# Weight units of an attention stage made in pieces, one per attention head, with the sign of a number carried by the slope of a leaky activation

## The chip, the cores and the metric

The kernel runs on one core of one Trainium2 chip. A core has five engines that run side by side and each take their own instructions in order: TensorE (PE in the profile; it multiplies matrices, and its weight loads are listed as PEld), VectorE (DVE), ScalarE (ACT), GpSimd (POOL) and SyncE (SP), which here issues all the transfers between the chip's memory (HBM) and the on-chip memory (SBUF). PSUM is the small memory into which TensorE writes its results; it has eight banks. Engines wait for each other by semaphores.

The metric is the time of one execution in microseconds (us) on the device. The kernel before took 622.03 us, the median of 3 runs (620.55 to 623.03).

## The reference

Three stages follow one another. q, k and v have 2 batches, 12 heads, 448 positions and a head size of 64, so there are 24 heads in all. The weights are float64 in memory, and the result is float32.

```python
def _attn_ref(q, k, v):                      # causal attention, all 24 heads
    scores = scale * np.matmul(q, k.transpose(0, 1, 3, 2))
    scores = np.where(mask, -1000000000.0, scores)
    attn = np.exp(scores - np.max(scores, axis=-1, keepdims=True))
    attn = attn / (np.sum(attn, axis=-1, keepdims=True) + 1e-09)
    return np.matmul(attn, v)
def _moe_ref(x, w_gate, w_val, w_out):       # 896 x 768, inner size 1536
    g = x @ w_gate
    silu = g * (1.0 / (1.0 + np.exp(-g)))
    val = x @ w_val
    return silu * val @ w_out
def _moe2_ref(x, w_in, w_out):               # 896 x 768, inner size 2048
    h = x @ w_in
    return (h * np.clip(h + 3.0, 0.0, 6.0) / 6.0) @ w_out
```

## The kernel before

**Precision.** A float32 product is made from three products of shortened numbers: each operand is split into a high part (float32r) and the rest. So every weight tile exists as `whi` and `wlo`.

**Weight units.** The weights are handled in 68 units of 128 x 768 numbers. `w_unit` makes one: SP loads the raw float64 bits (`raw`, 768 KB); ScalarE multiplies the upper word, read as a float32, by 2^-112 (L96), VectorE shifts the result left by 3 (L99), which throws the sign away, puts the sign bit back from the upper word (L100) and adds the top bits of the lower word (L103); ScalarE rounds to `whi` (L108), and GpSimd subtracts for `wlo` (L109). L100 and L103 both read two SBUF tiles, `raw` and `w`.

**Attention.** `attention()` goes through the heads in steps t = 0 to 27, one head per step, as a pipeline: in step t TensorE makes the scores of head t (`sc`, L315), the transposes of the probabilities of head t-1 (`tp`, L358) and the product with v of head t-2 (`pv`, L386). `weave` deals these products out in turn, so that TensorE's order is fixed by hand. In even steps the q and k of the next pair of heads are turned as well (`turn_parts`: four `kn` and four `qn` transposes, L241, copies `f` by ScalarE, CASTs by VectorE into `kk` and `qq` (L254), subtractions by GpSimd for the rest (L255), and for the keys two copies by transfer per head (L260)). In odd steps the finished outputs are turned (`xt_parts`, L420). For the scores of each head VectorE makes four reductions (L328, the tile `e`, one for each of the widths 336, 112, 224 and 448, in this order) and ScalarE four exponentials (L338). TensorE's transposes in step t+1 begin with the block of width 112 that comes from step t. Between the 336 and the 112 reduction stands the copy `et` (L364).

**Order.** A scheduler orders each engine's instructions by its own estimate of times, except those that are pinned to program order. Of the attention's weight units, the first instruction (L96) is pinned, the load is not. Three units are made in the attention stage, whole, after steps 20, 23 and 26 (`UNIT_AT`).

**MLPs.** `mlps()` then uses the units in order, two units ahead of use; all its products are matmuls of L168 and L529.

Of the kernel before, what the change touches and what calls it, by code (L numbers as in the profile page):

```python
# [8 lines left out]
F32 = mybir.dt.float32  # L9
F32R = mybir.dt.float32r  # L10
U32 = mybir.dt.uint32
AF = mybir.ActivationFunctionType
ALU = mybir.AluOpType
# [11 lines left out]
AHEAD = 2  # L25
SOON = 200
LATE = 2
UNIT_AT = (20, 23, 26)
GROUPS = ((2,), (0, 1), (3,))

@with_exitstack
def tile_attention_glu_mlp(
# [17 lines left out]
    nc = tc.nc  # L50
# [7 lines left out]
    KD = DM // 128  # L58
# [21 lines left out]
    def bank(use):  # L80
        n = idle.pop(0)
        return banks.tile([128, 512], F32, tag=f"bank{n}", name=f"{use}_{n}"), n


    def w_unit(src, a, b):
        def slot(tag, shape, dt, n, m):
            i = made_n[tag] = made_n.get(tag, -1) + 1
            i %= m if more else n
            return (ring if i < n else more[0]).tile(shape, dt, tag=f"{tag}{i}", name=f"{tag}{i}")

        raw = slot("raw", [128, a, b, 2], U32, RAW, RAW + 1)
        nc.sync.dma_start(out=raw.rearrange("p a b two -> p a (b two)"), in_=src)
        low, high = raw[:, :, :, 0], raw[:, :, :, 1]
        w = ring.tile([128, a, b], F32, tag="w", name="w", bufs=2)
        wu = w.bitcast(U32)
        first = nc.scalar.activation(out=w, in_=high.bitcast(F32), func=AF.Copy, scale=2.0**-112)  # L96
        if in_attention:
            tc.keep_in_program_order(first)
        nc.vector.tensor_scalar(out=wu, in0=wu, scalar1=3, scalar2=None, op0=ALU.logical_shift_left)  # L99
        nc.vector.scalar_tensor_tensor(  # L100
            out=wu, in0=high, scalar=0x80000000, in1=wu, op0=ALU.bitwise_and, op1=ALU.bitwise_or
        )
        nc.vector.scalar_tensor_tensor(  # L103
            out=wu, in0=low, scalar=29, in1=wu, op0=ALU.logical_shift_right, op1=ALU.bitwise_or
        )
        hi = slot("whi", [128, a, b], F32R, WB, WB + 1)
        lo = slot("wlo", [128, a, b], F32R, WB, WB + 1)
        nc.scalar.copy(hi, w)  # L108
        nc.gpsimd.tensor_tensor(out=lo, in0=w, in1=hi.bitcast(F32), op=ALU.subtract)  # L109
        return hi, lo  # L110

    def cols(w, j, n=128):
        w = w.bitcast(U32)
# [2 lines left out]
    units = []  # L116
# [13 lines left out]
    made = []  # L130
    made_n = {}
    more = []
    in_attention = [1]
    used = [0]

    def prefetch(n):
        while len(made) < min(n, len(units)):
            made.append(w_unit(*units[len(made)]))

    def next_unit():  # L140
        u = used[0]
# [36 lines left out]
    def attention():  # L178
        with ExitStack() as st:
# [9 lines left out]
                out=mask[:, S - C :], in_=mask[:, S - C :], pattern=[[-1, C]],  # L189
# [7 lines left out]
            for i in range(NV):  # L197
                t = fix.tile([C, 2, NC, D + 1], F32, name=f"v1_{i}")
# [8 lines left out]
            def load(p):  # L207
                if p >= NPAIR:
                    return
                b, hp = pairs[p]  # L210
                h0 = 2 * hp
                for src, dst, nm in ((k, natk, "kn"), (q, natq, "qn")):
                    t = nat.tile([C, NC, 2, D], F32, tag=nm, name=nm)
                    for j in range(2):
                        nc.sync.dma_start(  # L215
                            out=t[:, :, j, :], in_=src[b, h0 + j].rearrange("(c p) d -> p c d", p=C)
                        )
                    dst[p] = t

            def load_v(p):  # L220
                if p >= NPAIR:
                    return
                b, hp = pairs[p]
                vt = vset[p % NV]
                nc.sync.dma_start(
                    out=vt.rearrange("p j c d -> p (j c) d")[:, :, :D],
                    in_=v[b, 2 * hp : 2 * hp + 2].rearrange("j (c p) d -> p (j c) d", p=C),
                )

            def turn_parts(p):  # L230
                if p >= NPAIR:
                    return []
                t = sets[p % NSET]
                box = {}

                def one(src, c):
                    n = src[p]
                    if c == 0:
                        box["tr"] = bank("tr")
                    tr, bn = box["tr"]  # L240
                    nc.tensor.transpose(  # L241
                        tr[:, c * C : (c + 1) * C], n[:, c].rearrange("p j d -> p (j d)"), ident[:C, :C]
                    )
                    if c < NC - 1:
                        return
                    f = wk.tile([128, S], F32, tag="f", name="f")
                    nc.scalar.copy(f, tr[:, :S])
                    idle.append(bn)
                    hi, lo = (t["qq"], t["qq"]) if src is natq else (t["kk"], t["k2"])
                    for j in range(2):  # L250
                        r = slice(j * 64, j * 64 + 64)
                        o = slice(64 - j * 64, 128 - j * 64)
                        lr = o if src is natq else r
                        nc.vector.tensor_copy(hi[r, j, :], f[r, :])  # L254
                        nc.gpsimd.tensor_tensor(  # L255
                            out=lo[lr, j, :], in0=f[r, :], in1=hi[r, j, :].bitcast(F32), op=ALU.subtract
                        )
                        if src is natk:
                            for w in (hi, lo):
                                nc.sync.dma_start(out=w[o, j, :].bitcast(F32), in_=w[r, j, :].bitcast(F32))  # L260

                return [lambda src=src, c=c: one(src, c) for src in (natk, natq) for c in range(NC)]

            def first_turn():

                t = sets[0]
                got = {}
                for nm, src in (("k", natk), ("q", natq)):
                    got[nm] = bank("tr")
                    for c in range(NC):  # L270
                        nc.tensor.transpose(
                            got[nm][0][:, c * C : (c + 1) * C],
                            src[0][:, c].rearrange("p j d -> p (j d)"),
                            ident[:C, :C],
                        )
                kt, qt = (got[nm][0][:, :S] for nm in "kq")

                def head(j):
                    r = slice(j * 64, j * 64 + 64)
                    o = slice(64 - j * 64, 128 - j * 64)  # L280
                    kk, k2, qq = (t[nm][:, j, :] for nm in ("kk", "k2", "qq"))
                    nc.vector.tensor_copy(kk[r], kt[r])
                    nc.vector.tensor_tensor(out=k2[r], in0=kt[r], in1=kk[r].bitcast(F32), op=ALU.subtract)
                    nc.scalar.copy(qq[r], qt[r])
                    nc.gpsimd.tensor_copy(kk[o], kk[r].bitcast(F32))
                    nc.vector.tensor_tensor(out=qq[o], in0=qt[r], in1=qq[r].bitcast(F32), op=ALU.subtract)
                    nc.scalar.copy(k2[o], k2[r].bitcast(F32))
                    if j == 1:
                        idle.extend(n for _, n in got.values())

                head(0)
                return [lambda: head(1)]
# [136 lines left out]
            def weave(*lists):  # L429
                marked = sorted(  # L430
                    ((i + 0.5) / len(l) + 1e-3 * k, k, i) for k, l in enumerate(lists) for i in range(len(l))
                )
                for _, k, i in marked:
                    lists[k][i]()
# [2 lines left out]
            load(1)  # L437
            load_v(0)
            second = first_turn()
            for t in range(0, NH + 4):  # L440
                turns_now = []
                if t % 2 == 0:
                    nxt = t // 2 + 1
                    turns_now = turn_parts(nxt)
                    load(nxt + 1)
                    load_v(nxt)
                if t % 2 == 1:
                    turns_now = xt_parts((t - 5) // 2)
                weave(sc_parts(t), tp_parts(t - 1), pv_parts(t - 2), turns_now, second)
                second = []  # L450
                if t in UNIT_AT:
                    prefetch(UNIT_AT.index(t) + 1)

    def mlps():
        in_attention.clear()
        more.append(ctx.enter_context(tc.tile_pool(name="more", bufs=1)))
        gpool = ctx.enter_context(tc.tile_pool(name="gpool", bufs=1))

# [29 lines left out]
        for e in range(KD):  # L488
            got = [bank("mm") for _ in PARTS]
            pts = [t[:, : part.stop - part.start] for (t, _), part in zip(got, PARTS)]  # L490
            for hh in range(2):
                wh, wl = next_unit()
                for pt, part in zip(pts, PARTS):
# [3 lines left out]
                        first=hh == 0,  # L497
# [37 lines left out]
        for eh in range(2):  # L535
            got = [bank("mm") for _ in range(TT)]
            acc = [t[:, :EH] for t, _ in got]
            for g in range(NG - LATE):
                w = next_unit()
# [15 lines left out]
            idle.extend(n for _, n in got)  # L555

    attention()
    mlps()


# [28 lines left out]
```

## Time and profile before

| | us |
|---|---|
| median of 3 runs | 622.03 |
| the profiled execution: its own time | 623.78 |
| the profiled execution: span, first to last instruction | 622.0 |
| TensorE busy in the span | 610.7 (98%) |
| VectorE busy | 344.8 (55%) |
| ScalarE busy | 265.2 (43%) |
| GpSimd busy | 185.6 (30%) |

The attention stage takes the first 123 us of the span, the two MLPs the rest. The table's shares are means over both: a share of 55% for VectorE says nothing of the attention stage, where it is much higher. What matters for a change in one stage is which wait ends last there, and that is read from the timeline of that stage, engine by engine. A step's start is read from the first score product of the step (L315, 128x336).

### The profile page before, as it was taken

The numbers are of one execution on the slowest core, as the hardware profiler recorded it, in microseconds if no ns is written. First come the engines' busy times: TensorE is split into PE (matmuls) and PEld (weight loads), VectorE is DVE, ScalarE is ACT, GpSimd is POOL, SyncE is SP. The second block draws the span as 40 slices with busy tenths as digits, with TensorE's granted clock in tenths as the row PEclk, the third lists the DMA queues.
The fourth block names the chain that finished last, engine by engine and source line by source line (L and its number), as shares of the span: only waits on it lengthen the run. The fifth ranks groups of instructions, "written<-read, shape, count | busy, mean of one in ns | idle before, by whom it ended". The sixth has DMA issues, their size and how long they took to land.

```text
span 622.0 us, 9356 instructions
## 1 busy us (share of the span) xinstructions
PE 610.7 (98%) x3600; PEld 565.9 (91%) x3600; DVE 344.8 (55%) x687; ACT 265.2 (43%) x450; POOL 185.6 (30%) x125
## 2 busy tenths in 40 slices
PE   6999998999999999999999999999999999999997
PEld 5999998989988889998888999888899999999997
DVE  5788889669855544444544343566666543325101
ACT  5777777544443334333322323554555442223100
POOL 4456655025322222322222232222223222213200
PEclk9999999799999999999999999999999999999999
DMA  9665542146543333333333334333334433352002
GB/s 179 187 158 130 140 112 70 44 152 203 156 149 103 102 103 115 127 112 101 102 101 102 108 117 127 106 103 102 101 103 110 126 119 101 102 166 77 0 1 89
DMA packets 83916, 70.14 MB, mean 113 GB/s; under 512 B 35232, under 2 KB 79776, under 8 KB 83872
## 3 DMA queue, kind: packets, MB, share of 16 engines
q1 hardware_dynamic: 83872, 69.55, 38.9%
q8 instruction: 28, 0.46, 0.3%
q14 instruction: 16, 0.13, 0.1%
HBM read 61.73 MB, written 2.75 MB: 104 GB/s over the span
## 4 chain that ended last, share of the span: by engine, by line
PE 93%; DVE 3%; DMA 1%; ACT 1%; SPq 1%; issue 0%; ACTq 0%; DVEq 0%
PE mm L168 60%; PE mm L529 19%; PE pv L386 5%; PE sc L315 4%; PE tp L358 3%; PE tr L241 1%; DMA kk<-kk 1%; PE tr L420 1%; DVE e L328 1%; SPq L215 1%; DMA qn<-in_q_dram 1%; DVE qq L254 1%; DVE w L100 0%; DVE w L103 0%; ACT e L338 0%
## 5 line engine op out<-in xcount | busy, mean ns | idle before, releaser
L109 POOL TENSOR_TENSOR wlo<-w,whi 128x768 fp32r<-128x768 f32 x68 | 128.0, 1884 | 359.1 <-ACT whi L108 298.4
L99 DVE TENSOR_SCALAR w<-w 128x768 uint32<-128x768 uint32 x68 | 38.7, 570 | 156.0 <-ACT w L96 155.7
L108 ACT CAST whi<-w 128x768 fp32r<-128x768 f32 x68 | 56.9, 839 | 124.1 <-PE mm L168 83.7
L168 PE MATMUL mm<-x1l,whi 128*128 128x384 f32 (+1 forms) x288 | 104.9, 364 | 0.2 <-DVE x1l L151 0.2
L168 PE MATMUL mm<-x1h,wlo 128*128 128x384 f32 (+1 forms) x288 | 104.9, 364 | 0.0
L96 ACT ACTIVATE w<-raw 128x768 f32<-128x768 f32 x68 | 61.3, 902 | 101.4 <-POOL wlo L109 98.9
L168 PE MATMUL mm<-x1h,whi 128*128 128x384 f32 (+1 forms) x288 | 104.5, 363 | 0.0
L103 DVE SCALAR_TENSOR_TENSOR w<-raw,w 128x768 uint32<-128x768 uint32 x68 | 74.6, 1097 | 1.0
L386 PE MATMUL pv<-v,et 112*112 112x65 f32 x480 | 75.2, 246 | 0.0
L529 PE MATMUL mm<-whi,gl 128*128 128x384 f32 x224 | 74.8, 334 | 0.0
L529 PE MATMUL mm<-whi,gh 128*128 128x384 f32 x224 | 74.8, 334 | 0.0
L529 PE MATMUL mm<-wlo,gh 128*128 128x384 f32 x224 | 74.8, 334 | 0.0
L168 PE MATMUL mm<-x2h,wlo 128*128 128x384 f32 (+1 forms) x192 | 70.0, 364 | 0.0
L168 PE MATMUL mm<-x2l,whi 128*128 128x384 f32 (+1 forms) x192 | 69.8, 364 | 0.0
L168 PE MATMUL mm<-x2h,whi 128*128 128x384 f32 (+1 forms) x192 | 69.6, 362 | 0.0
L386 PEld LDWEIGHTS pv<-v,et 112*112 112x112 f32 x480 | 67.8, 182 | 1.6
L100 DVE SCALAR_TENSOR_TENSOR w<-raw,w 128x768 uint32<-128x768 uint32 x68 | 65.9, 968 | 1.6
L358 PE MATMUL tp<-ident,e 112*112 112x112 f32 x240 | 63.3, 272 | 2.2 <-ACT e L338 2.0
L168 PEld LDWEIGHTS mm<-x1l,whi 128*128 128x128 f32 x288 | 54.0, 188 | 6.5 <-DVE x1l L151 0.5
L168 PEld LDWEIGHTS mm<-x1h,whi 128*128 128x128 f32 x288 | 54.1, 188 | 6.2 <-ACT x1h L150 0.2
L168 PEld LDWEIGHTS mm<-x1h,wlo 128*128 128x128 f32 x288 | 54.0, 188 | 5.6
L338 ACT ACTIVATE e<-e,m 112x336 f32<-112x336 f32 (+1 forms) x96 | 48.8, 532 | 22.7 <-DVE m L328 22.7
(69 smaller groups left out, 1050.0 us busy)
## 6 DMA issues: line engine op xcount, KB each, us to landing
raw<-in_moe_w_out_dram SPq DMA_DIRECT2D x28, 768.0 KB, 4.3
raw<-in_moe_w_in_dram SPq DMA_DIRECT2D x16, 768.0 KB, 4.5
raw<-in_moe_w_gate_dram SPq DMA_DIRECT2D x12, 768.0 KB, 4.3
raw<-in_moe_w_val_dram SPq DMA_DIRECT2D x12, 768.0 KB, 4.3
kn<-in_k_dram SPq DMA_DIRECT2D x24, 112.0 KB, 2.9
qn<-in_q_dram SPq DMA_DIRECT2D x24, 112.0 KB, 2.6
v<-in_v_dram SPq DMA_DIRECT2D x12, 224.0 KB, 3.1
out_dram<-ob SPq DMA_DIRECT2D x14, 192.0 KB, 1.8
```

Of the source, the lines that this page charges most:

```text
L96: first = nc.scalar.activation(out=w, in_=high.bitcast(F32), func=AF.Copy, scale=2.0**-112)
L99: nc.vector.tensor_scalar(out=wu, in0=wu, scalar1=3, scalar2=None, op0=ALU.logical_shift_left)
L100: nc.vector.scalar_tensor_tensor(out=wu, in0=high, scalar=0x80000000, in1=wu, op0=ALU.bitwise_and, op1=ALU.bitwise_or)
L103: nc.vector.scalar_tensor_tensor(out=wu, in0=low, scalar=29, in1=wu, op0=ALU.logical_shift_right, op1=ALU.bitwise_or)
L108: nc.scalar.copy(hi, w)
L109: nc.gpsimd.tensor_tensor(out=lo, in0=w, in1=hi.bitcast(F32), op=ALU.subtract)
L168: lambda lhs=lhs, rhs=rhs, i=i: nc.tensor.matmul(ps, lhs, rhs, start=(first and i == 0), stop=(last and i == total - 1))
L315: nc.tensor.matmul(sp[:C, o : o + w], t["qq"][:, j, c * C : (c + 1) * C], t[("kk", "k2")[i]][:, j, 0:w], start=(i == 0), stop=(i == 1),)
L338: nc.scalar.activation(out=es, in_=es, func=AF.Exp, scale=-1.0, bias=m[:, x : x + 1])
L358: nc.tensor.transpose(tp[:C, at - lo : at - lo + C], e[:, at : at + C], ident[:C, :C])
L386: nc.tensor.matmul(box["o"][:, qc, :], et[:, at : at + C], vt[:, j, c, :], start=(c == 0), stop=(c == qc))
L529: nc.tensor.matmul(acc, lhs[:, tsl], rhs[:, i, :], start=(fc == 0 and n == 0), stop=(fc == K2 - 1 and n == 2),)
```

## The change

Three things change. First, the scaling by ScalarE becomes a leaky activation with the slope 2^32 for negative numbers: a negative number comes out with 32 more in its exponent, and the shift left by 3 moves just this bit to the place of the sign. The VectorE instruction that put the sign back (L100) is gone, in all 68 units. Second, units in the attention stage are made in pieces: the first two in 6 pieces of 128 columns, the third in 2 of 384. After each step at most one piece (or the load) is emitted. Third, the units start after steps 11, 18 and 25; their load, their scaling and their shift are pinned to program order.

```diff
-UNIT_AT = (20, 23, 26)
+UNIT_AT = (11, 18, 25)
...
-        first = nc.scalar.activation(out=w, in_=high.bitcast(F32), func=AF.Copy, scale=2.0**-112)
-        if in_attention:
-            tc.keep_in_program_order(first)
-        nc.vector.tensor_scalar(out=wu, in0=wu, scalar1=3, scalar2=None, op0=ALU.logical_shift_left)
-        nc.vector.scalar_tensor_tensor(
-            out=wu, in0=high, scalar=0x80000000, in1=wu, op0=ALU.bitwise_and, op1=ALU.bitwise_or
-        )
...
+        def load():
+            first = nc.sync.dma_start(out=raw.rearrange("p a b two -> p a (b two)"), in_=src)
+            if pieces > 1:
+                tc.keep_in_program_order(first)
+
+        def piece(k):
+            p = slice(k * a // pieces, (k + 1) * a // pieces)
+            low, high, wu = raw[:, p, :, 0], raw[:, p, :, 1], w[:, p].bitcast(U32)
...
+            first = nc.scalar.activation(
+                out=w[:, p], in_=high.bitcast(F32), func=AF.Prelu, scale=2.0**-112, alpha=2.0**32
+            )
+            if pieces > 1:
+                tc.keep_in_program_order(first)
+            shift = nc.vector.tensor_scalar(out=wu, in0=wu, scalar1=3, scalar2=None, op0=ALU.logical_shift_left)
+            if pieces > 1:
+                tc.keep_in_program_order(shift)
+            nc.vector.scalar_tensor_tensor(
+                out=wu, in0=low, scalar=29, in1=wu, op0=ALU.logical_shift_right, op1=ALU.bitwise_or
+            )
+            nc.scalar.copy(hi[:, p], w[:, p])
+            nc.gpsimd.tensor_tensor(out=lo[:, p], in0=w[:, p], in1=hi[:, p].bitcast(F32), op=ALU.subtract)
...
                 if t in UNIT_AT:
-                    prefetch(UNIT_AT.index(t) + 1)
+                    pieces += w_unit(*units[len(made)], pieces=KD if len(made) < 2 else 2)
+                if pieces:
+                    pieces.pop(0)()
```

A piece that is emitted after step t runs in step t+1: the first unit's pieces in steps 13 to 18, the second's in steps 20 to 25. All lines of the kernel move down by 13 (L254 becomes L267, L328 becomes L341); L99 becomes L114, L103 becomes L117, L109 becomes L121 and the load L92 becomes L100.

The first place is VectorE in step 21, an odd step, from the reciprocal to the 112 reduction; before:

```order
L398 RECIPROCAL ri<-r 112x4
L254 CAST qq_98<-f 64x448 x2
L399 TENSOR_TENSOR xn<-pv_1572,ri 112x4x64
L328 ISA e,m<-sc_1668,mask 112x336
L328 ISA m 112x1
L364 COPY et<-tp_1666 112x336
L99 TENSOR_SCALAR w<-w 128x768
L100 SCALAR_TENSOR_TENSOR w<-raw_1650,w 128x768
L328 ISA e,m<-sc_1680,mask 112x112
```

The same place on VectorE now:

```order
L411 RECIPROCAL ri<-r 112x4
L267 CAST qq_98<-f 64x448 x2
L412 TENSOR_TENSOR xn<-pv_1617,ri 112x4x64
L341 ISA e,m<-sc_1707,mask 112x336
L341 ISA m 112x1
L114 TENSOR_SCALAR w<-w 128x128
L377 COPY et<-tp_1705 112x336
L117 SCALAR_TENSOR_TENSOR w<-raw_1542,w 128x128
L341 ISA e,m<-sc_1719,mask 112x112
```

The piece stands where the whole unit stood, one of its two instructions ahead of the copy `et` and one behind it, and still in front of the 112 reduction. Steps 13, 15 and 17 now read the same; before they had no weight instructions.

The second place is GpSimd, over the same part of the attention stage; before, three pairs of heads and then the first unit:

```order
L255 TENSOR_TENSOR k_94<-f,kk_93 64x448 x2
L255 TENSOR_TENSOR qq_92<-f,qq_92 64x448 x2
L255 TENSOR_TENSOR k_97<-f,kk_96 64x448 x2
L255 TENSOR_TENSOR qq_95<-f,qq_95 64x448 x2
L255 TENSOR_TENSOR k_100<-f,kk_99 64x448 x2
L255 TENSOR_TENSOR qq_98<-f,qq_98 64x448 x2
L109 TENSOR_TENSOR wlo_1658<-w,whi_1657 128x768
```

GpSimd now, in steps 15 to 17:

```order
L268 TENSOR_TENSOR qq_98<-f,qq_98 64x448 x2
L121 TENSOR_TENSOR wlo_975<-w,whi_974 128x128
L268 TENSOR_TENSOR k_94<-f,kk_93 64x448
L121 TENSOR_TENSOR wlo_975<-w,whi_974 128x128
L268 TENSOR_TENSOR k_94<-f,kk_93 64x448
L268 TENSOR_TENSOR qq_92<-f,qq_92 64x448 x2
```

One piece of an odd step stands ahead of the two key subtractions, and one of an even step between them.

The third place is SP, which issues the transfers; before, the second unit's load stood here, in step 4:

```order
L225 DMA v_0_101<-in_v_dram 112x8x64
L92 DMA raw_1838<-in_moe_w_val_dram 128x6x256
L260 DMA kk_93<-kk_93 64x448
L260 DMA k_94<-k_94 64x448
L260 DMA kk_93<-kk_93 64x448
L260 DMA k_94<-k_94 64x448
L215 DMA kn<-in_k_dram 112x4x64 x2
```

SP now, where the first unit is loaded, behind the key copies of step 10:

```order
L273 DMA kk_93<-kk_93 64x448
L273 DMA k_94<-k_94 64x448
L273 DMA kk_93<-kk_93 64x448
L273 DMA k_94<-k_94 64x448
L100 DMA raw_972<-in_moe_w_gate_dram 128x6x256
L228 DMA qn<-in_q_dram 112x4x64 x2
L238 DMA v_1_103<-in_v_dram 112x8x64
L228 DMA kn<-in_k_dram 112x4x64 x2
```

The load stood right ahead of a pair's key copies; now it stands right behind them, with the input loads of later pairs behind it. TensorE's order is the same as before but for two places of a few rows.

## Rows read from the trace of the kernel before

**Rows 1.** Waits, whole span: engine, line, what for; us, times, longest

```profile
PE tp L358 <- ACT e L338: 2.0, 2, 1.6
```

**Rows 2.** Windows: stretch, length, busy time (instructions) by engine, clock, DMA, GB/s

```profile
65.48:74.27 8.79, 8.79 (x91) 8.60 (x90) 7.81 (x30) 6.65 (x16) 4.98 (x5) 1.00 0.56 129
...
108.54:115.27 6.73, 6.73 (x36) 6.41 (x37) 3.55 (x15) 3.37 (x7) 1.53 (x1) 0.50 0.32 110
...
304.00:618.50 314.50, 314.50 (x1652) 293.79 (x1651) 138.20 (x198) 107.74 (x160) 73.80 (x40) 1.00 0.33 99
```

**Rows 3.** Timeline of TensorE, steps 5, 17, 18, 21, 22: start, length, instruction, [idle before]

```profile
29.72 0.39 PE L315 MATMUL sc<-kk,qq 128*112 128x336 f32 x1
34.47 0.38 PE L315 MATMUL sc<-kk,qq 128*112 128x336 f32 x1 [0.30 <-DMA kk<-kk]
...
83.07 0.39 PE L315 MATMUL sc<-kk,qq 128*112 128x336 f32 x1
...
87.28 0.39 PE L315 MATMUL sc<-kk,qq 128*112 128x336 f32 x1
...
100.67 0.39 PE L315 MATMUL sc<-kk,qq 128*112 128x336 f32 x1
...
106.57 0.31 PE L358 MATMUL tp<-ident,e 112*112 112x112 f32 x1 [1.57 <-ACT e L338]
106.67 0.38 PE L315 MATMUL sc<-kk,qq 128*112 128x336 f32 x1
```

**Rows 4.** Timeline of VectorE in step 17, an odd step without a unit

```profile
83.61 1.12 DVE L254 CAST qq<-f 64x448 fp32r<-64x448 f32 x2
...
85.52 0.50 DVE L364 COPY et<-tp 112x336 f32<-112x336 f32 x1
86.13 0.28 DVE L328 CUSTOM_DVE_ANT_0 e<-sc,mask 112x112 f32<-112x112 f32 x1
```

**Rows 5.** Timeline of VectorE in step 21, with the first unit

```profile
103.54 0.55 DVE L99 TENSOR_SCALAR w<-w 128x768 uint32<-128x768 uint32 x1
104.12 1.78 DVE L100 SCALAR_TENSOR_TENSOR w<-raw,w 128x768 uint32<-128x768 uint32 x1
105.83 0.26 DVE L328 CUSTOM_DVE_ANT_0 e<-sc,mask 112x112 f32<-112x112 f32 x1
```

**Rows 6.** Timeline of GpSimd, steps 17 and 21 (two instructions in a row)

```profile
84.38 2.56 POOL L255 TENSOR_TENSOR qq<-f,qq 64x448 fp32r<-64x448 f32 x2 [0.33 <-DVE qq L254]
...
101.98 3.10 POOL L255 TENSOR_TENSOR qq<-f,qq 64x448 fp32r<-64x448 f32 x2 [0.32 <-DVE qq L254]
```

**Rows 7.** Single lines, whole span: ns min/median/max of one, first and last start

```profile
L99 DVE TENSOR_SCALAR w<-w x68: 543/560/1239, 103.5 to 578.7; 128x768 uint32<-128x768 uint32 x68
L100 DVE SCALAR_TENSOR_TENSOR w<-raw,w x68: 948/959/1778, 104.1 to 579.2; 128x768 uint32<-128x768 uint32 x68
L109 POOL TENSOR_TENSOR wlo<-w,whi x68: 1819/1843/2484, 108.2 to 590.4; 128x768 fp32r<-128x768 f32 x68
L255 POOL TENSOR_TENSOR qq<-f,qq x22: 1132/1243/1679, 11.9 to 103.4; 64x448 fp32r<-64x448 f32 x22
```

**Rows 8.** Groups by form, 60 to 100 us: count, busy us, mean ns, idle before

```profile
L338 ACT ACTIVATE e<-e,m 112x112 f32<-112x112 f32 x10 | 3.9, 389 | 1.9 <-DVE m L328 1.9
L396 DVE TENSOR_SCALAR r<-pv 112x4 f32<-112x4 f32 x9 | 1.5, 163 | 1.6 <-PE pv L386 1.6
```

**Rows 9.** Timeline of SP in step 4

```profile
26.44 0.55 SPq L92 DMA_DIRECT2D raw<-in_moe_w_val_dram  x1
```

**Rows 10.** Chain that ended last: start, us, piece

```profile
28.28 6.05 DMA kk<-kk
```

**Rows 11.** DMA issues, whole span: count, KB each, median us to landing

```profile
raw<-in_moe_w_val_dram SPq DMA_DIRECT2D x12, 768.0 KB, 4.3
```

**Rows 12.** Timeline of TensorE, first unit of the MLPs

```profile
130.03 0.47 PE L168 MATMUL mm<-x1h,whi 128*128 128x512 f32 x1
130.67 0.50 PE L168 MATMUL mm<-x1l,whi 128*128 128x512 f32 x1 [0.16 <-DVE x1l L151]
```

More of the change, by code (lines that the diff above doesn't have):

```diff
@@ L82, in bank, with w_unit @@
         return banks.tile([128, 512], F32, tag=f"bank{n}", name=f"{use}_{n}"), n
-    def w_unit(src, a, b):
+    def w_unit(src, a, b, pieces=1):
         def slot(tag, shape, dt, n, m):
@@ L91, in w_unit @@
         raw = slot("raw", [128, a, b, 2], U32, RAW, RAW + 1)
-        nc.sync.dma_start(out=raw.rearrange("p a b two -> p a (b two)"), in_=src)
-        low, high = raw[:, :, :, 0], raw[:, :, :, 1]
         w = ring.tile([128, a, b], F32, tag="w", name="w", bufs=2)
-        wu = w.bitcast(U32)
-        first = nc.scalar.activation(out=w, in_=high.bitcast(F32), func=AF.Copy, scale=2.0**-112)
-        if in_attention:
-            tc.keep_in_program_order(first)
-        nc.vector.tensor_scalar(out=wu, in0=wu, scalar1=3, scalar2=None, op0=ALU.logical_shift_left)
-        nc.vector.scalar_tensor_tensor(
-            out=wu, in0=high, scalar=0x80000000, in1=wu, op0=ALU.bitwise_and, op1=ALU.bitwise_or
-        )
-        nc.vector.scalar_tensor_tensor(
-            out=wu, in0=low, scalar=29, in1=wu, op0=ALU.logical_shift_right, op1=ALU.bitwise_or
-        )
         hi = slot("whi", [128, a, b], F32R, WB, WB + 1)
         lo = slot("wlo", [128, a, b], F32R, WB, WB + 1)
-        nc.scalar.copy(hi, w)
-        nc.gpsimd.tensor_tensor(out=lo, in0=w, in1=hi.bitcast(F32), op=ALU.subtract)
-        return hi, lo
+        made.append((hi, lo))
+        def load():
[18 more added lines that the diff above has]
+            nc.gpsimd.tensor_tensor(out=lo[:, p], in0=w[:, p], in1=hi[:, p].bitcast(F32), op=ALU.subtract)
+        return [load] + [lambda k=k: piece(k) for k in range(pieces)]
     def cols(w, j, n=128):
@@ L132, in tile_attention_glu_mlp @@
     more = []
-    in_attention = [1]
     used = [0]
@@ L137, in prefetch @@
         while len(made) < min(n, len(units)):
-            made.append(w_unit(*units[len(made)]))
+            for step in w_unit(*units[len(made)]):
+                step()
     def next_unit():
@@ L439, in attention @@
             second = first_turn()
+            pieces = []
             for t in range(0, NH + 4):
@@ L451, in attention @@
                 if t in UNIT_AT:
-                    prefetch(UNIT_AT.index(t) + 1)
+                    pieces += w_unit(*units[len(made)], pieces=KD if len(made) < 2 else 2)
+                if pieces:
+                    pieces.pop(0)()
+            for step in pieces:
+                step()
     def mlps():
-        in_attention.clear()
         more.append(ctx.enter_context(tc.tile_pool(name="more", bufs=1)))
```

## The prediction

> **What bounds the kernel now.** I read the windows first, then the waits, then the timelines of single engines around the longest wait. In the windows TensorE is busy for all of a pair of attention steps (8.79 of 8.79 us) and for all of the MLPs' long stretch (314.50 of 314.50), while VectorE has 0.98 us free in a pair of steps (8.79 less 7.81) [rows 2]. So TensorE sets the time in both stages, and another engine counts only where TensorE waits for it. The waits name one such place of weight: the transposes wait for the exponentials for 2.0 us in all, 1.6 of them in one piece [rows 1]. TensorE's timeline puts that piece at 106.57, at the end of step 21, the step in which the first weight unit is made. Step 21 lasts from 100.67 to 106.67, which is 6.00 us; step 17, also odd and with no unit in it, lasts from 83.07 to 87.28, which is 4.21 [rows 3]. Behind the wait the granted clock is 0.50, the lower level of 1.2 GHz, from 108.54 to 115.27 [rows 2]. In steps 13 and 14, with TensorE busy throughout, it is 1.00, the upper level of 2.4 GHz [rows 2].
>
> Why TensorE waited is seen on VectorE. In step 17 the 112 reduction starts at 86.13, just behind the copy `et` [rows 4]; carried over by the 17.60 us between the two steps' starts, it would stand at 103.73 in step 21. There it starts at 105.83, behind the unit's shift and L100 [rows 5]: 2.10 late. TensorE's next step was 1.79 late, so this reduction has an allowance of 0.31.
>
> L100 took 1.78 there; its median is 0.959 [rows 5, 7]. GpSimd was in its two `qq` subtractions until 101.98 + 3.10 = 105.08 [rows 6], and L100 ended at 105.90, 0.82 behind that. I read this as: a VectorE instruction with two SBUF inputs stands still while GpSimd subtracts.
>
> **What the change takes away.** Four terms.
> - Step 21 without its whole unit: 6.00 - 4.21 = 1.79.
> - The clock's fall that followed: 6.73 us at half speed cost 6.73 / 2 = 3.37.
> - The second unit's load, issued at 26.44, stood ahead of the key copies; the copy of 28.28 took 6.05 [rows 9, 10], and step 5 lasted 34.47 - 29.72 = 4.75 against 4.21, with TensorE released by that copy [rows 3]: 0.54. The load now stands behind a step's key copies. A load lands 4.3 after its issue [rows 11], and the next key copies come a pair of steps (8.79) later. The `qn`, `v` and `kn` loads behind it on SP land later by up to 4.3, and are for pairs that are turned a pair of steps later. So I cost it at nothing; if that cover fails, it is another 0.54 each for two loads.
> - The start of the MLPs: two products stand 0.64 apart with 0.16 idle, waiting for VectorE, which had two whole units to make there [rows 12]. Now the first two units are done by then and only the third, in two pieces, is left: between 0.16 and 0.5, I take 0.3.
>
> Sum: 6.0. L100 itself, 68 times 0.959 of VectorE, brings nothing more in the MLPs, since TensorE waits there for nothing.
>
> **What it adds.** A piece is a shift and an L117 on VectorE, two instructions on ScalarE and one on GpSimd, in steps 13 to 18 and 20 to 25. No row shows them, so I bound them by the nearest: a VectorE instruction of 4 columns takes 0.163 [rows 8], the shift of 768 columns 0.560, L100 0.959 [rows 7]. On the line between, 128 columns take 0.23 and 0.29. Two pieces in a pair of steps are 1.04; each instruction begins some 0.07 before its forerunner's record ends (105.83 against 105.90), so 0.76 of room is taken out of 0.98. ScalarE has 8.79 - 6.65 = 2.14 free, and four instructions, each at most the 0.389 of the smallest exponential [rows 8], take 1.56. By quantity the pieces fit.
>
> By place they do not. In odd steps L117 stands behind `et` and in front of the 112 reduction, and this is when GpSimd is in the `qq` subtractions: in step 17 from 84.38 to 86.94 [rows 6]. The shift can go between the two of them and pushes the second one back by its 0.23, to 87.17. What is left of L117 then is the 0.82 less 640 columns at (0.959 - 0.163) / 764 us, so 0.15, and the reduction begins 0.07 before its end: 87.25 instead of 86.13, which is 1.12 late. Less the allowance TensorE stops for 0.81. So it goes in step 13. From step 15 on there is the even step's piece on GpSimd as well, between the two key subtractions. 448 columns take at least 1.132 and 768 take 1.819 [rows 7], so 128 take 0.45. The `qq` CASTs stand behind the key subtractions in time, and they take 1.12 for two [rows 4], which I read as waiting for these. I pass the 0.45 on in full (the other end is not at all): 1.57 late, 1.26 stopped, in steps 15, 17 and 21. In step 19 there is no piece, and from step 22 on no pair is turned, so GpSimd is free. Sum: 0.81 + 3 x 1.26 = 4.6. In even steps L117 comes when GpSimd is idle: nothing.
>
> Both ends of this term: nothing, if short instructions slip in between GpSimd's, and 4 x 1.57 + 0.6 for even steps, about 6.9, if the allowance is used up.
>
> The Trainium skill (SBUF — State Buffer, section "SBUF: two separate sides") says more: the port pair that the two engines share is an exclusive lock, and whoever starts first keeps it for the whole instruction. Step 21 agrees as to L100, but not as to the shift: the second subtraction is recorded from 103.4 and took 1.679 instead of 1.132 [rows 7], and the shift that began later, at 103.54, took its usual 0.55 [rows 5]. By the rule the shift would wait as well, and the sum would be the third rival's.
>
> **The sum.** -6.0 + 4.6 = -1.4. The profiled execution took 623.78 (span 622.0 and 1.8 around it), so 622.4 for such a one; it stands 1.75 above the median of the runs, and from that, 622.03, the forecast is 620.6.
>
> **Rivals.**
> - The pieces cost nothing: GpSimd lets the short L117 in between its two subtractions, and the lateness stays below 0.31. For it: VectorE's room of 0.98, and that the shift did get in. Against: the 0.82 behind GpSimd's end. Time: 622.03 - 6.0 = 616.0.
> - The clock falls again, which makes it slower than before. The place is the boundary behind steps 15, 17 and 21, where TensorE would stop for 1.26; a stop of 1.57 was followed by the lower clock, at a price of 3.37. Against it: that stop was longer, and the 0.30 in step 5 had no fall behind it. One fall gives 624.0, two 627.3, three 630.7: from the second on it is slower.
> - GpSimd always goes first: in every odd step the shift too waits for the second subtraction, and only then come `et` (0.50 long [rows 4]) and L117, each 0.07 less for its follower. For step 13 that is 86.94 + 0.16 + 0.43 + 0.22 = 87.75, 1.62 late instead of 1.12. Four steps at 0.50 more: 620.6 + 2.0 = 622.6, no change.
>
> **How the numbers follow.** What a measurement of this kernel can tell from no change is about 0.5%, 3.1 us: faster is below 618.9, slower above 625.1. The forecast has 0.40, with its own range 618 to 622.5, of which 0.06 lies below 618.9. The first rival has 0.33, all of it faster. The second has 0.20: 0.16 with two falls or more, slower, 0.04 with one, the same. The third has 0.05, the same. The other 0.02, split between faster and slower, is for a cause that I do not see. Faster: 0.06 + 0.33 + 0.01 = 0.40; the same: 0.34 + 0.04 + 0.05 = 0.43; slower: 0.17. The range goes from just below the first rival, 615.4, to just under two falls, 626.8, which leaves out the worse half of the second rival and a little at the low end.
>
> **What would show it.** In the timeline of VectorE the odd steps 13, 15, 17 and 21 should have an L117 of some 0.8 us that ends 0.1 to 0.2 behind GpSimd's second `qq` subtraction, and the even steps one of 0.3. On TensorE the steps behind these should start late by 0.8, 1.3, 1.3 and 1.3, released by ScalarE's exponential, and step 5 should last 4.2. The clock should stay at the upper level from the early steps to the end; one stretch at 0.50 speaks for the second rival. L117 of 0.3 in odd steps, with odd steps of 4.2, makes the first rival right and the forecast wrong. Stops in even steps, or a wait for `raw`, would mean that I have the place wrong.

## The result and the profile after

The changed kernel took 625.2 us, the median of 16 runs (623.50 to 627.52); the kernel before took 620.48 beside it (619.29 to 624.27). The ratio is 1.0056, with a 95% interval of 1.0042 to 1.0071: slower by about half a per cent, where I had forecast 0.2% faster. Timed a second time it was 1.0052 (1.0028 to 1.0075). The time is inside the stated range, but the forecast was on the wrong side of the kernel before.

The execution that was profiled took 626.45 (span 624.7). The windows of six steps show where it went: step 5, odd steps 13 and 15, even step 16, and steps 20 and 21. Columns are those of [rows 2].

```profile
29.87:34.09 4.22, 4.22 (x45) 4.12 (x44) 3.96 (x16) 2.90 (x8) 3.64 (x3) 1.00 0.56 134
65.08:69.87 4.79, 4.44 (x45) 4.20 (x44) 4.69 (x18) 3.36 (x9) 3.76 (x4) 1.00 0.95 186
74.47:79.79 5.32, 4.43 (x45) 4.19 (x44) 5.22 (x18) 3.35 (x10) 4.21 (x5) 1.00 0.57 136
79.79:84.39 4.60, 4.60 (x48) 4.51 (x48) 4.29 (x18) 4.20 (x12) 1.64 (x3) 1.00 0.45 104
98.81:106.13 7.32, 5.09 (x48) 4.64 (x48) 4.07 (x17) 3.93 (x11) 1.25 (x1) 0.98 0.38 112
106.13:113.34 7.21, 7.21 (x43) 6.98 (x44) 5.36 (x18) 4.25 (x11) 4.57 (x6) 0.55 0.58 167
```

Four of these are as forecast in kind: step 5 is down to 4.22 from the 4.75 of [rows 3]; steps 13 and 15 are 0.58 and 1.11 longer than the 4.21 of an odd step without a unit; the even step 16 is at its 4.60. Step 20, an even step, is not: it lasts 7.32, with TensorE idle for 2.23 of it. Step 21 then has TensorE busy throughout and still takes 7.21, at a granted clock of 0.55. These two steps are what I had not seen.

TensorE's timeline names the waits, before the ends of steps 13, 15 and 17 and inside step 20. They answer to the last but one row of [rows 3].

```profile
69.77 0.31 PE L371 MATMUL tp<-ident,e 112*112 112x112 f32 x1 [0.35 <-ACT e L351]
...
79.69 0.31 PE L371 MATMUL tp<-ident,e 112*112 112x112 f32 x1 [0.89 <-ACT e L351]
...
89.60 0.31 PE L371 MATMUL tp<-ident,e 112*112 112x112 f32 x1 [0.86 <-ACT e L351]
...
104.37 0.41 PE L399 MATMUL pv<-v,et 112*112 112x65 f32 x2 [0.99 <-DVE et L377]
...
106.01 0.43 PE L371 MATMUL tp<-ident,e 112*112 112x112 f32 x1 [1.24 <-ACT e L351]
```

The 1.57 of step 21 is gone, and in its place there are three stops of 0.35 to 0.89 and two that add up to 2.23. The two are followed back on the other engines: first ScalarE in step 20, then VectorE.

```profile
103.32 0.31 ACT L109 ACTIVATE w<-raw 128x128 f32<-128x128 f32 x1 [2.87 <-DMA raw<-in_moe_w_val_dram]
103.54 0.52 ACT L260 COPY f<-tr 128x448 f32<-128x448 f32 x1
```

```profile
103.67 0.23 DVE L114 TENSOR_SCALAR w<-w 128x128 uint32<-128x128 uint32 x1 [3.14 <-ACT w L109]
103.81 0.50 DVE L377 COPY et<-tp 112x336 f32<-112x336 f32 x1
```

ScalarE stands 2.87 at the first piece of the second unit, because the weights have not landed. Its place in ScalarE's order is fixed, so the copy `f` stands behind it. VectorE stands 3.14 at the shift that needs the piece, with the copy `et` behind it, for which TensorE's `pv` waits. The chain of waits tells when the load went out and how long it took:

```profile
94.68 1.16 POOL k L268
95.83 0.02 issue
95.85 0.46 SPq L273
96.31 0.05 issue
96.36 6.93 DMA raw<-in_moe_w_val_dram
```

GpSimd's second key subtraction releases the key copy on SP (L273), and the load stands behind that copy on SP's queue. It is issued at 96.36, in the middle of step 19, and lands 6.93 later.

The mechanism that I did forecast is seen in step 17, on VectorE (to be read against [rows 4]) and on GpSimd ([rows 6]):

```profile
84.93 1.64 DVE L267 CAST qq<-f 64x448 fp32r<-64x448 f32 x2
...
87.36 0.28 DVE L114 TENSOR_SCALAR w<-w 128x128 uint32<-128x128 uint32 x1
87.56 0.49 DVE L377 COPY et<-tp 112x336 f32<-112x336 f32 x1
87.98 0.95 DVE L117 SCALAR_TENSOR_TENSOR w<-raw,w 128x128 uint32<-128x128 uint32 x1
88.85 0.26 DVE L341 CUSTOM_DVE_ANT_0 e<-sc,mask 112x112 f32<-112x112 f32 x1
```

```profile
84.22 0.45 POOL L121 TENSOR_TENSOR wlo<-w,whi 128x128 fp32r<-128x128 f32 x1
84.75 1.14 POOL L268 TENSOR_TENSOR k<-f,kk 64x448 fp32r<-64x448 f32 x1
86.22 2.56 POOL L268 TENSOR_TENSOR qq<-f,qq 64x448 fp32r<-64x448 f32 x2 [0.33 <-DVE qq L267]
```

The two CASTs took 1.64 instead of 1.12, since GpSimd has its 0.45 of `wlo` between the key subtractions; L117 took 0.95 instead of the 0.28 that it takes in even steps, and ended at 88.93, 0.15 behind the end of GpSimd's `qq` subtractions (86.22 + 2.56 = 88.78).

### The profile page after: what moved, and what is told of

It reads as the page before. It is cut to its first block, busy times and chain, and to the rows that moved or that the text cites. A ratio compares the mean times of both kernels' runs of the same rounds, so it can differ in the third digit from the quotient of the medians.

```text
span 624.7 us, 9353 instructions
## 1 busy us (share of the span) xinstructions
PE 610.4 (98%) x3600; PEld 565.8 (91%) x3600; DVE 286.4 (46%) x641; ACT 267.9 (43%) x472; POOL 184.2 (29%) x136
## 4 chain that ended last, share of the span: by engine, by line
PE 93%; DVE 3%; DMA 2%; SPq 1%; ACT 1%; issue 0%; POOL 0%; DVEq 0%; ACTq 0%
PE mm L181 60%; PE mm L546 19%; PE pv L399 5%; PE sc L328 4%; PE tp L371 3%; PE tr L254 1%; DMA raw<-in_moe_w_val_dram 1%; DVE qq L267 1%; DVE e L341 1%; PE tr L433 1%; SPq L228 1%; DMA qn<-in_q_dram 1%; DVE w L117 0%; ACT e L351 0%; DVE et L377 0%
## 5 line engine op out<-in xcount | busy, mean ns | idle before, releaser
L121 POOL TENSOR_TENSOR wlo<-w,whi 128x768 fp32r<-128x768 f32 (+2 forms) x79 | 127.5, 1614 | 361.8 <-ACT whi L120 299.9
L114 DVE TENSOR_SCALAR w<-w 128x768 uint32<-128x768 uint32 (+2 forms) x79 | 41.4, 524 | 197.1 <-ACT w L109 196.8
L120 ACT CAST whi<-w 128x768 fp32r<-128x768 f32 (+2 forms) x79 | 59.0, 746 | 131.6 <-PE mm L181 87.9
L109 ACT ACTIVATE w<-raw 128x768 f32<-128x768 f32 (+2 forms) x79 | 63.0, 799 | 99.7 <-POOL wlo L121 94.9
L117 DVE SCALAR_TENSOR_TENSOR w<-raw,w 128x768 uint32<-128x768 uint32 (+2 forms) x79 | 73.5, 931 | 1.8
L181 PE MATMUL mm<-gh,wlo 128*128 128x384 f32 (+1 forms) x144 | 52.5, 364 | 0.0
```

The source lines that it names most:

```text
L109: first = nc.scalar.activation(out=w[:, p], in_=high.bitcast(F32), func=AF.Prelu, scale=2.0**-112, alpha=2.0**32)
L114: shift = nc.vector.tensor_scalar(out=wu, in0=wu, scalar1=3, scalar2=None, op0=ALU.logical_shift_left)
L117: nc.vector.scalar_tensor_tensor(out=wu, in0=low, scalar=29, in1=wu, op0=ALU.logical_shift_right, op1=ALU.bitwise_or)
L120: nc.scalar.copy(hi[:, p], w[:, p])
L121: nc.gpsimd.tensor_tensor(out=lo[:, p], in0=w[:, p], in1=hi[:, p].bitcast(F32), op=ALU.subtract)
L181: lambda lhs=lhs, rhs=rhs, i=i: nc.tensor.matmul(ps, lhs, rhs, start=(first and i == 0), stop=(last and i == total - 1))
```

## The experiments

Theory A, formed from this trace: the loss is (1) the second unit's load, which lands after its first piece is due, and the clock's fall behind that stop, and (2) the odd steps' pieces, of which one part is L117 held up by GpSimd's `qq` subtraction and the other is the `wlo` piece passed on through the CASTs. Rivals stand in the expectations. The names are those of the changed kernel, with its lines moved down by 1 to 10 in the variants; slope_only has those of the kernel before, moved up by 3 behind the line that is gone. In the cuts of code, `...` stands for lines left out.

**load_early: the second unit's load two steps earlier.**

```
 UNIT_AT = (11, 18, 25)          # from here a unit's pieces are taken
+LOAD_AT = (11, 16, 25)          # here its load is issued
...
```

> The changed kernel, with the second unit's load issued behind the key copies of step 16 instead of step 18; pieces and places as changed. Theory A (two separate losses: a late load, and L117 in the wrong place): step 20, 7.32 us in the changed kernel, goes back to 4.6, 2.7 us less, and the half-clock stretch behind it goes; the odd steps 15, 17 and 21 keep some 5.3 and step 13 some 4.8. Time against the changed kernel's 625.2: 2.7 to 4 less, so 621 to 622.5, about that of the kernel before. Theory B (VectorE simply has no room for the pieces, and the wait for the load only fell into time that would be lost anyway): step 20 stays above 6, time 624 to 625.

Measured: 621.86 median, ratio to before 0.9997 (0.9978 to 1.0016), a granted clock of 1.00 in all 12 runs. Windows of steps 17, 20 and 21:

```profile
83.34:88.66 5.32, 4.45 (x46) 4.21 (x44) 5.22 (x18) 3.35 (x10) 4.22 (x5) 1.00 0.69 191
97.76:102.35 4.59, 4.59 (x47) 4.49 (x48) 4.14 (x17) 4.18 (x12) 1.50 (x2) 1.00 0.30 70
102.35:107.64 5.29, 4.44 (x46) 4.20 (x44) 5.19 (x18) 3.36 (x9) 4.18 (x5) 1.00 0.65 174
```

Step 20 is back at 4.59 and step 21 at 5.29 with the clock up: part (1) of the theory holds. The load stands elsewhere on its queue here, so this run alone doesn't tell whether its reader or its place did the harm. The odd steps stay long, which is part (2).

**wait_moved: the load where the change put it, the first piece one step later.**

```
-UNIT_AT = (11, 18, 25)
+LOAD_AT = (11, 18, 25)
+UNIT_AT = (11, 19, 25)          # second unit's pieces in steps 21 to 26
...
```

> The changed kernel with the second unit's load where it is there (behind step 18's key copies), but its first piece one step later, in step 21 instead of 20. Theory A (nothing is wrong with the load but that its first piece stands at the head of ScalarE before the data has landed): whether the load lands after 4.8 or 6.9, ScalarE and VectorE wait for raw by no more than 0.3; step 20 lasts 4.6 instead of 7.32, step 21 4.8 to 5.3 with the clock at 1.00, and the time is 621 to 622, like load_early's. Rival (the load at this place pushes other loads of the attention late, v above all, which took 5.9 there instead of 2.9): step 20 stays above 5.5 whatever its pieces do, and the time stays above 623.

Measured: 621.02, ratio 0.9992 (0.9976 to 1.0008). Windows of steps 20 and 21:

```profile
98.45:103.04 4.59, 4.59 (x48) 4.49 (x48) 3.80 (x15) 3.79 (x10) 1.53 (x2) 1.00 0.66 193
103.04:107.81 4.77, 4.43 (x45) 4.19 (x44) 4.67 (x18) 3.35 (x9) 3.74 (x4) 1.00 0.68 185
```

The load is issued at the same place of step 19, and with its reader later nothing waits for it: step 20 is at 4.59. The rival, in which it pushes other loads late, is not seen, in this execution nor in the ten times (619.81 to 621.82). But the load landed after 4.7 in the one that was profiled, so what a landing of 6.9 would do to the loads behind it no trace here shows. Step 21 is at 4.77, as step 13 is, since no `wlo` piece stands before it; that makes about 0.5 of what this run gains on the changed kernel.

**after_again: the changed kernel once more, on the same chip as wait_moved.** No edit.

> The changed kernel once more, beside it on the same chip. Both theories: 625.2 as before, or 623.5 to 624 in an execution whose clock is 1.00 throughout. What the profile is to tell is whether the second unit's load takes about 6.9 to land again and step 20 about 7.3 (then that landing belongs to this place), or under 5 with step 20 at about 5.3 (then the late landing was an accident of one execution).

Measured: 624.11 (621.95 to 627.87). The profiled execution was one of the fastest, 622.2. Its steps 20 and 21 in windows, and ScalarE's wait:

```profile
98.47:103.55 5.08, 4.83 (x47) 4.59 (x48) 4.06 (x17) 3.92 (x11) 1.23 (x1) 1.00 0.53 158
103.55:109.11 5.56, 4.49 (x44) 4.20 (x44) 5.20 (x18) 3.53 (x10) 4.45 (x6) 1.00 0.67 176
```

```profile
100.75 0.32 ACT L109 ACTIVATE w<-raw 128x128 f32<-128x128 f32 x1 [0.64 <-DMA raw<-in_moe_w_val_dram]
```

This is nearer to the second outcome: the load landed after 4.70, and step 20 lasted 5.08. But the piece still waited 0.64, so it is late in both profiled executions, and by how much changes from one to the next. Step 20 was 0.49 too long instead of 2.73, and the clock did not fall. How often a landing takes as long as 6.93 the times don't tell. Over both timings the 26 runs of the changed kernel spread from 621.95 to 627.87, with 7 of them at a clock of 1.00 (622.2 to 623.95).

**early_wlo: load_early, with GpSimd's `wlo` pieces behind the two `qq` subtractions.**

```
-            nc.gpsimd.tensor_tensor(out=lo[:, p], in0=w[:, p], in1=hi[:, p].bitcast(F32), op=ALU.subtract)
+            rests.append(rest)   # rest() issues it, with its place kept
...
+                while rests:     # behind the pair's qq subtractions
+                    rests.pop(0)()
```

> load_early, with GpSimd's subtraction of a piece (wlo) put behind the two qq subtractions of the next pair instead of between the key subtractions; it then falls beside no CAST of qq. Theory A (the stop in an odd step has two parts: L117 held up by GpSimd's second qq subtraction, about 0.6, and the 0.45 of the wlo piece passed on through the CASTs, about 0.5): the two CASTs take 1.12 again instead of 1.64, steps 15, 17 and 21 last 4.75 to 4.85 like step 13 instead of 5.3, TensorE's waits there fall from 0.87 to about 0.35, and the time is about 1.5 less than load_early's. Rival (the CASTs are slow for another reason, or VectorE's own quantity makes the step long): steps 15, 17 and 21 stay at 5.2 to 5.3 and the time is load_early's.

Measured: 619.09, ratio 0.9954 (0.9935 to 0.9973), beside 0.9997 of load_early. GpSimd, then the window of step 17:

```profile
81.12 2.57 POOL L278 TENSOR_TENSOR k<-f,kk 64x448 fp32r<-64x448 f32 x2 [3.03 <-DVE kk L277]
84.02 2.56 POOL L278 TENSOR_TENSOR qq<-f,qq 64x448 fp32r<-64x448 f32 x2 [0.33 <-DVE qq L277]
86.65 0.94 POOL L123 TENSOR_TENSOR wlo<-w,whi 128x128 fp32r<-128x128 f32 x2
```

```profile
82.61:87.50 4.89, 4.45 (x45) 4.21 (x44) 4.79 (x18) 3.35 (x9) 4.38 (x5) 1.00 0.77 202
```

The CASTs took 1.22 instead of 1.66, and steps 15, 17, 19 and 21 lasted 4.92, 4.89, 4.19 and 4.78 instead of 5.33, 5.32, 4.52 and 5.29. So the `wlo` piece costs 0.33 to 0.51 in each of these four, 1.7 in all. The medians, from two chips, differ by more, 2.8. The times on record account for most of the other 1.1: load_early's 12 runs fall into five of 620.35 to 620.74 and seven of 621.80 to 622.36, with its median among the seven, while eight of early_wlo's 12 lie between 618.66 and 619.18. The medians of the two lower groups are 1.8 apart, the two profiled executions (one of each lower group) 2.0. What makes the groups stays open.

**short_q: load_early, with q's low part subtracted in 8 columns only.**

```
+                        n = 8 if src is natq else S
-                            out=lo[lr, j, :], in0=f[r, :], in1=hi[r, j, :].bitcast(F32), op=ALU.subtract
+                            out=lo[lr, j, :n], in0=f[r, :n], in1=hi[r, j, :n].bitcast(F32), op=ALU.subtract
```

> load_early, with q's low part subtracted in its first 8 columns only (the others stay zero from a memset at the start; that part of the computation is left out), so that GpSimd is idle when the odd step's L117 comes; VectorE's own work is what it was. Theory A (L117 waits for GpSimd's second qq subtraction): L117 of odd steps takes 0.3 instead of 0.94, TensorE doesn't stop in steps 13, 15, 17 and 21, which last 4.2 to 4.3, and the time is 3 to 4 less than load_early's. Rival (quantity: VectorE has too much to do in front of the 112 reduction, whatever GpSimd does): L117 may fall, but the odd steps stay above 4.6.

Measured: 620.12, ratio 0.9970 (0.9951 to 0.9988). It leaves out part of the work, and its start is longer by 2.3 with the memsets in it, so the steps decide, not the total. L117 (here L118) in step 17, and the windows of steps 13 and 17:

```profile
87.85 0.28 DVE L118 SCALAR_TENSOR_TENSOR w<-raw,w 128x128 uint32<-128x128 uint32 x1
```

```profile
66.30:70.49 4.19, 4.19 (x45) 4.09 (x44) 4.07 (x18) 3.28 (x9) 1.91 (x4) 1.00 0.94 187
...
84.33:89.02 4.69, 4.46 (x46) 4.22 (x44) 4.59 (x18) 3.26 (x9) 2.34 (x5) 1.00 0.69 163
```

With GpSimd idle, L117 takes 0.28 in an odd step too, and step 13, which has no `wlo` piece before it, is at the 4.19 of a step without a unit. My expectation for steps 15 to 21 (4.2 to 4.3) was wrong: this kernel still has the `wlo` pieces between the key subtractions, its CASTs still took 1.6, and steps 15, 17 and 21 lasted 4.64 to 4.69 (step 19, without a piece, 4.66). Read together with early_wlo, the 1.1 of such a step divides into some 0.65 for L117 (5.32 - 4.69 = 0.63 in step 17) and some 0.43 for `wlo` (5.32 - 4.89). The rival by quantity falls on step 13: VectorE has the same instructions there and TensorE doesn't stop.

**both_moved: load_early, with each odd step's piece woven in behind the reductions.**

```
-UNIT_AT = (11, 18, 25)
+UNIT_AT = (12, 18, 25)
...
+                piece = [lambda: None, pieces.pop(0)] if pieces and t % 2 == 1 else []
-                weave(sc_parts(t), tp_parts(t - 1), pv_parts(t - 2), turns_now, second)
+                weave(sc_parts(t), tp_parts(t - 1), pv_parts(t - 2), turns_now, second, piece)
```

> As load_early, and in odd steps the piece stands behind the 112, 224 and 448 reductions instead of in front of them; even steps' pieces stay in their place. The work on VectorE is the same to the instruction. Theory A (place): odd steps 13, 15, 17 and 21 go back to 4.2 to 4.4, no stop of TensorE over 0.3; time 617 to 618.5. Theory B (quantity): the odd steps keep 5.3 or the loss shows up in the even steps; time 621 to 622.5 as in load_early.

Measured: 621.04, ratio 0.9990 (0.9972 to 1.0007). Starts of steps 15, 16 and 17 on TensorE:

```profile
72.86 0.38 PE L331 MATMUL sc<-kk,qq 128*112 128x336 f32 x1
...
77.61 0.38 PE L331 MATMUL sc<-kk,qq 128*112 128x336 f32 x1
...
82.55 0.38 PE L331 MATMUL sc<-kk,qq 128*112 128x336 f32 x1
```

Theory A missed, and what came is what theory B foretold: L117 takes 0.28 everywhere, but a pair lasts 9.69 (4.75 + 4.94) beside 9.92 in load_early and 8.79 in [rows 2], with the loss spread over both steps. The CASTs still took 1.72, so part of it is the `wlo` piece. In the even steps the shift took 0.42 to 0.44 instead of 0.23, each time beside a `wlo` piece on GpSimd, so that is another collision and not quantity. The rest stays open, and this run alone can't tell place from quantity.

**even_only and even_wlo: load_early with three pieces of 256 columns, in even steps alone; then with early_wlo's edit as well.**

```
-UNIT_AT = (11, 18, 25)
+UNIT_AT = (12, 18, 25)
...
-                    unit = w_unit(*units[len(made)], pieces=KD if len(made) < 2 else 2)
+                    unit = w_unit(*units[len(made)], pieces=KD // 2 if len(made) < 2 else 2)
-                elif pieces:
+                elif pieces and t % 2 == 1:
                     pieces.pop(0)()
```

> As load_early, but the first two units are made in 3 pieces of 256 columns each, all of them in even steps (14 to 24), when GpSimd is idle; odd steps have none. Theory A: L117 takes some 0.42 in all steps, odd steps 4.2, even steps 4.6 to 4.8; time 617 to 618.5, like both_moved. Theory B (quantity): twice the work in the even steps, which then last 5 or more; time 620 to 622.

> even_only, with the same edit: the wlo pieces of 256 columns stand behind the two qq subtractions. Theory A: even_only's odd steps of 4.65 hold no piece, so what is left there is the wlo piece of 0.73 passed on through the CASTs; the CASTs take 1.12 again, odd steps 4.2 to 4.35, TensorE waits for no exponential in them, and the time is 1 to 2 less than even_only's, about 616.5. Rival (odd steps are long since VectorE as a whole is full, 9.3 a pair): a pair stays at 9.3 and the time is even_only's.

Measured: even_only 618.15, ratio 0.9953 (0.9937 to 0.9969), with a pair at 9.31. even_wlo 617.7 (616.86 to 618.31), ratio 0.9922 (0.9896 to 0.9948). Windows of two pairs of even_wlo, steps 15 to 16 and 17 to 18:

```profile
72.71:81.52 8.81, 8.81 (x91) 8.62 (x90) 8.37 (x32) 7.01 (x18) 5.60 (x5) 1.00 0.54 126
81.52:90.48 8.96, 8.96 (x91) 8.75 (x90) 8.35 (x32) 7.15 (x18) 5.70 (x6) 1.00 0.77 195
```

A pair with a third of a unit in it lasts 8.81 and 8.96, against 8.79 without, and TensorE is busy for all of it. The odd steps are at 4.20 to 4.33, as expected; the time is less below even_only's than expected (0.45 by the medians, from two chips). Of the versions that do all of the work, early_wlo, even_only and even_wlo lie clear of the kernel before, even_wlo furthest, at 0.8%; its slowest run, 618.31, is below the changed kernel's fastest, 621.95. Pieces of 256 columns are also fewer instructions on VectorE, so this run shows that the work fits, but does not alone show why.

**slope_only: the kernel before, with the sign carried by the slope and L100 gone, nothing else.**

```
-        first = nc.scalar.activation(out=w, in_=high.bitcast(F32), func=AF.Copy, scale=2.0**-112)
+        first = nc.scalar.activation(out=w, in_=high.bitcast(F32), func=AF.Prelu, scale=2.0**-112, alpha=2.0**32)
...
-            out=wu, in0=high, scalar=0x80000000, in1=wu, op0=ALU.bitwise_and, op1=ALU.bitwise_or
```

> The kernel before with the sign carried by the slope and L100 gone, and nothing else: whole units after steps 20, 23 and 26. If step 21's stop comes from the wait of an instruction with two SBUF inputs for GpSimd (A): the one that is left takes the place of the one that is gone and waits for the same subtraction, step 21 stays at 5.8 to 6.0, and the time is that of the kernel before within 0.8. If it comes from the amount of work (B): step 21 gets shorter by the 0.96 of the removed instruction, and the time by 1 or more. In both the MLPs gain nothing.

Measured: 621.01, ratio 0.9993 (0.9977 to 1.0010). VectorE in step 21, where L100 is now the one merge that is left, and TensorE:

```profile
102.56 1.77 DVE L100 SCALAR_TENSOR_TENSOR w<-raw,w 128x768 uint32<-128x768 uint32 x1
```

```profile
105.54 0.31 PE L355 MATMUL tp<-ident,e 112*112 112x112 f32 x1 [1.90 <-ACT e L335]
```

The remaining merge takes over the hold-up: 1.77 where L100 had 1.78 [rows 5], and TensorE stops for 1.90. Step 21 itself lasts 4.14 here and not the expected 5.8 to 6.0, because step 22's first score product stands ahead of the stop in this kernel's order; the stop falls into step 22. An instruction less on VectorE for each of 68 units brings nothing that can be measured.

## Why the prediction was wrong

**The step that failed is the load "costed at nothing".** I asked which loads the second unit's load would push late, and compared 4.3 with the 8.79 to the next key copies. What mattered was its own reader, the first piece on ScalarE. How little cover it has can be estimated from the trace of before, with one offset taken from the changed kernel. SP's key copy of that pair, and the start of step 20 on TensorE:

```profile
92.89 0.52 SPq L260 DMA_DIRECT2D k<-k  x1
```

```profile
96.07 0.39 PE L315 MATMUL sc<-kk,qq 128*112 128x336 f32 x1
```

A load behind this copy goes out at 92.89 + 0.52 = 93.41 and lands at 97.7. In the changed kernel ScalarE came to the piece at 103.32 - 2.87 = 100.45, 1.64 after the start of step 20; from 96.07 that is 97.7. By this estimate there was no spare at all, and every delay of the key subtractions (the 0.45 of `wlo` is one) moves the load and not its reader. With a landing of 4.70 the piece waited 0.64, with 6.93 it waited 2.87. Taking the wait away in two ways gives 0.9997 and 0.9992 instead of 1.0056 and 1.0052. It costs some 0.6%, which is up to 3.7 us of the 4.6 between the forecast and the median; wait_moved and after_again, beside each other on one chip, are 3.1 apart (621.02 and 624.11), and 0.5 of that is step 21 without its `wlo` piece. In the profiled execution it is 7.32 - 4.59 = 2.73 in step 20 and 7.21 - 5.29 = 1.92 in step 21, where the clock fell.

**The term for the clock was mis-sized.** I took 3.37 for the fall off a profiled execution of 623.78 and subtracted all of it from a median. Of 76 later runs of the kernel before, 19 have a granted clock of 0.999 or more, with a median of 620.1; 24 have 0.997 and 620.9; 33 have less and 622.8. The median of all, 621.7, holds some 1.6 of it. Counted from the runs without a fall, the other terms give 620.1 - 2.6 + 4.6 = 622.1; load_early, which has them all and no late load, took 621.86. So 1.8 of the 3.37 was taken off too much.

**The odd steps were right in kind and a little too high.** Forecast were stops of 0.81 in step 13 and 1.26 in steps 15, 17 and 21; the steps of load_early are longer than 4.21 by 0.58, 1.12, 1.11 and 1.08. Two sizes were off. The shift did not push GpSimd's second subtraction back: the two took 2.56 with it, as without it in [rows 6], because it fell on the end of the first (see the third rival below). So L117 was held up by some 0.2 less. And the `wlo` piece, passed on in full as I had taken it, reaches step 19 too, which has no piece of its own and lasted 4.52: 0.31 that I left out. In sum 4.2 instead of 4.6.

**The other terms held.** Step 5 lasted 4.22 (4.21 forecast). From the start of step 22 to the end of the span it took 624.7 - 113.34 = 511.4, and in the kernel before 622.0 - 106.67 - 3.37 = 512.0 without the fall: 0.6 less over that stretch, where I took 0.3 for the start of the MLPs; where in the stretch it lies was not followed up. The even steps cost nothing (4.60), and L100's absence from the MLPs brought nothing that slope_only could show. Together the late load (3.1 to 3.7), the clock (1.8), the odd steps (-0.4) and the MLPs (-0.3) make 4.2 to 4.8, and the measured time is 4.6 above the forecast.

**The rivals.** The first, that the pieces cost nothing, falls with the odd steps of 4.79 to 5.32. The clock did fall again, but not where I put it: no fall came behind the stops of 0.9 in steps 15 and 17, and the one of the profile came with two stops of 2.23 together in step 20, for a reason that I did not have. Step 21 was 1.92 longer by it and not 3.37; at the lower clock TensorE no longer stopped in that step (busy for 7.21 of 7.21).

The third, that the shift waits for the second subtraction, did not come, but not because the shift is spared. In step 17 GpSimd's first `qq` subtraction ended at 87.56 and the second began at 87.63; the shift, from 87.36 to 87.64, fell on the place between the two. It took 0.28 there, in an even step 0.23. The other odd steps read the same. Where a shift begins in the middle of a subtraction, it waits, as in the MLPs of the changed kernel:

```profile
147.37 1.85 POOL L121 TENSOR_TENSOR wlo<-w,whi 128x768 fp32r<-128x768 f32 x1 [1.87 <-issue]
148.57 1.07 DVE L114 TENSOR_SCALAR w<-w 128x768 uint32<-128x768 uint32 x1
```

This shift took 1.07 instead of 0.56 and ended 0.42 behind the subtraction; the longest one of [rows 7], 1.239, also stands beside a `wlo`. In step 21 of the kernel before it was the subtraction that waited: its 1.679 is 0.55 above the shortest, 1.132, and 0.55 is the length of the shift. So the prediction's "not as to the shift" holds only of the order (the shift was recorded 0.13 later and yet went first); that the two exclude each other, the trace shows there too. On this the Trainium skill (SBUF — State Buffer, section "SBUF: two separate sides") is borne out. It says that a VectorE instruction with two SBUF inputs, or one in a two-port mode, and a GpSimd one shut each other out for a whole instruction (with two inputs, only where the GpSimd one reads SBUF). L117, with two inputs, ran 0.95 beside the subtraction and 0.28 without it. The shift has one input; that it runs in a two-port mode no run here shows directly, but it waits as the rule says of such an instruction.

## What to carry to other kernels

When a load is moved, look first for its own reader: take the issue of the instruction that it stands behind on its queue, add the landing, and compare that with the time at which the reader's engine comes to it, above all where the reader's place in its engine's order is fixed. A stop that lowers the clock is in part of the runs only; take such a term from several runs sorted by their granted clock, and not from one profile. Pieces of side work are cheap where the engine with which they collide is idle: nine steps that last 39.4 without a piece (five of 4.21 and four of 4.59) lasted 43.61 in load_early, and 39.88 in even_wlo, whose pieces avoid GpSimd's subtractions on both engines. And an instruction that seems to be spared by a collision may only have come at a gap: look for the same instruction elsewhere in the trace before a rule is drawn from it.

## What the runs showed of the hardware

The same 768 KB transfer at the same place landed after 6.93 in one execution and 4.70 in another. The windows of the slow one show a long tail (the last two columns are the DMA share and GB/s):

```profile
99.60:101.10 1.50, 1.50 (x19) 1.50 (x18) 0.93 (x3) 0.85 (x2) 0.00 (x0) 1.00 1.06 296
101.10:103.30 2.20, 2.20 (x22) 1.97 (x20) 0.00 (x0) 0.00 (x0) 0.00 (x0) 1.00 0.10 29
```

Most of it was there by 101.1, and in the last 2.2 us 29 GB/s were moved, at a DMA share of 0.10, which is 1.6 of the 16 engines. Why, I did not find out; `v`, issued at 98.10, was late with it (5.9, and 3.8 in the other execution). A median of landings (4.3 in [rows 11]) says nothing of such a tail, and the reader waits for the last byte.
